# Another place for v's last tokens, and both copies of the next q and k in front of the second exp

## The chip, the cores and the metric

The kernel runs on one core of one Trainium2 chip. The metric is the device time of one execution in microseconds, and of several runs the median. TensorE is PE in the profile (PEld its weight loads), VectorE is DVE, ScalarE is ACT, GpSimd is POOL, and SyncE is SP; every load and store of this kernel is issued by SP, in the order of its queue.

## The reference

Attention over a sliding window with a linear bias, and then a mixing layer in the frequency domain on its output. The inputs are q, k, v of 8 batches × 8 heads × 576 tokens × 64, 64 pairs of complex weights of 512 × 512, and one matrix `w_ch`, all in 32 bits.

```python
scores = q @ k.T / sqrt(64)                       # per batch and head
scores = where(0 <= i - j < 128, scores - slope[h] * |i - j|, -1e9)
x = softmax(scores) @ v                           # heads side by side: (8, 576, 512)
X = rfft(x, axis=1)[:, :64]                       # 64 modes
Y = X @ (w_r + 1j * w_i)                          # each mode has its own weights
u = x + irfft(Y, n=576)
out = u + relu(u @ w_ch)
```

## The kernel before

**Units and slots.** Attention is cut into 32 units, each a pair of heads `s` of a batch `b`. Group 0 is pair 0 of the 8 batches (units 0 to 7), group 1 is pairs 1 to 3 of every batch (units 8 to 31). Unit n is worked on in slot n by `_slot` (L596), which writes out by hand, for all engines at once, the order of their instructions; nothing reorders them afterwards. In slot n:

- PE computes the first half of the scores of unit n (`_score`, L481) into the one score buffer `sc`; then 18 transposes of q and 18 of k of unit n+1 (`_tr`, L453) into `tqk`; the product of attention and v of unit n−1 (`_av`, L531 to L540); weight tiles, if the slot has any (`_modes`, L671 and L675); the second half of the scores (L481, L490); a re-ordering of v (`_keys`, L437, into `vps`); and, at the last pair of a batch, the transform into the frequency domain (`_spectrum`, L581).
- ACT takes the exp of the first half (L495), copies the transposed q of unit n+1 out of PSUM (`_evac`, L461), takes the exp of the second half, and copies the transposed k.
- DVE multiplies the attention with the mask (L505), once for each half, copies `vps` to `vb` (L441) and divides the output of unit n−1 by its sums (L545 to L551).
- POOL casts q and k of unit n+2 (`_cast_qk`, L415) and v of unit n+1 (`_cast_v`, L422) to 16 bits, and multiplies the rest of the second half with its mask (`_mask3`, L510), which the last part of `_av` in the next slot needs.

`tqk` and `vps` take turns in two PSUM buffers. So the second group of transposes for unit n+2, in slot n+1, writes the buffer that `vps` of slot n held, once DVE has copied it.

**The last tokens of v.** Tokens 512 to 575 of v have a way of their own: for each pair of heads `_load_vt` (L375) issues two loads, `_vt` casts them on POOL (L400), brings them into order with 64 products on PE (L706, from `_vt` by way of `_pair`) and copies them to `vbt` on DVE (L407). Pair 0 is taken after slot 0, and pairs 1, 2 and 3 after slots 3, 4 and 5; for those three the mask is made first (`_mask`, L302). PE's products stand behind all of slot n's PE work, and in front of slot n+1's.

**The loads.** SP's queue begins with q, k and v of the units of group 0. Then come the six loads of the last tokens of pairs 1 to 3, and then, mixed with the q, k and v of further units, the weight tiles (`_load_w`, L636): a tile is two loads, `wr` and `wi`, of 768 KB each. Each of the two has a ring of `RING` = 3 slots. The six loads of last tokens go to one slot of the ring of `wr` (the tile `vtf`), and those of pair 0 to a tile of their own in `tmpc`, a pool of temporary tiles that also holds the constants' working tiles, `ang` and `kf` among them: the angles for the transform matrix `g.F`, which DVE computes and a Sin on ACT reads. A load waits on SP until the place that it writes is free; q and k have three batches of places and v has six.

**After attention.** Group 0's 22 weight tiles are used from slot 10 on, spread over the slots; group 1's 64 tiles stream after attention has ended, with `_xw`, `_ft` and `_z_early` beside them. `_finish` computes the output and stores it.

Of the kernel before, what the change touches and what calls it, by code (L numbers as in the profile page):

```python
# [9 lines left out]
FP32 = mybir.dt.float32  # L10
# [24 lines left out]
def kernel(  # L35
# [60 lines left out]
    with tc.manual_schedule(engines={ET.SP, ET.PE, ET.Activation, ET.DVE, ET.Pool}):  # L96
        with ExitStack() as wctx:
# [4 lines left out]
            with ExitStack() as actx:  # L102
                cp = actx.enter_context(tc.tile_pool(name="const", bufs=1))
                for j, grp in enumerate(GROUPS[:-1]):
                    g.X[j] = cp.tile([P, len(grp), 3, B, NM], BF16, name=f"X{j}")
                g.mask = cp.tile([P, NP, 2, 512], BF16)
                g.vbs = [cp.tile([P, 4, 2, 72], BF16, name=f"vb{i}") for i in range(3)]
                g.vbt = cp.tile([P, NP, B, 72], BF16)
                g.sel = cp.tile([P, 2, 2, 2, 64], BF16)
                g.qpool = actx.enter_context(tc.tile_pool(name="qk", bufs=QK))  # L110
                g.vpool = actx.enter_context(tc.tile_pool(name="v", bufs=VB))
                g.vts = actx.enter_context(tc.tile_pool(name="vts", bufs=2))
                g.work = actx.enter_context(tc.tile_pool(name="work", bufs=2))
                g.ps2 = actx.enter_context(
                    tc.tile_pool(name="ps2", bufs=1, space=bass.MemoryType.PSUM))
                g.ps1 = actx.enter_context(
                    tc.tile_pool(name="ps1", bufs=2, space=bass.MemoryType.PSUM))

                todo = list(tiles[0])
                n0 = g.first[1] + LA  # L120
                with tc.tile_pool(name="tmpc", bufs=1, side="right") as tp:
                    for n in range(n0):
                        if n == g.first[1]:
                            _load_w(g, 0, *todo.pop(0))
                        _load_qk(g, n)
                        if n < VB - 1:
                            _load_v(g, n)
                        elif n >= VB + 2:
                            _load_v(g, n - 3)
                        if n == 0:  # L130
                            for s in GROUPS[0]:
                                _load_vt(g, s, tp.tile([P, 2, 4 * g.D], FP32, name=f"vtf{s}"))
                        if n == g.first[1] - 1:
                            t = g.wpool.tile([P, ROWS, DM], FP32, tag="wr", name="vtf")
                            for i, s in enumerate(GROUPS[1]):
                                _load_vt(g, s, t[:, i].rearrange("p (h c) -> p h c", h=2))
                        if g.first[1] <= n < g.first[1] + RING - 1:
                            _load_w(g, 0, *todo.pop(0))
                    _consts(g, tp)
                    _cast_qk(g, 1)  # L140
                    _cast_v(g, 0)
                    _tr(g, 0, 0)
                    _tr(g, 0, 1)
                    _evac(g, 0, 0, nc.vector.tensor_copy)
                    _evac(g, 0, 1, nc.vector.tensor_copy)
                    for s in GROUPS[0]:
                        _mask(g, s)
                    _select(g)
                    todo_s = [(0, s) for s in GROUPS[0]] + [(3 + i, s) for i, s in enumerate(GROUPS[1])]
                    for n in range(g.first[1] - 1):  # L150
                        _slot(g, n, [], [])
                        for k, s in todo_s:
                            if k == n:
                                if s not in GROUPS[0]:
                                    _mask(g, s)
                                _vt(g, tp, s)
                zx = ctx.enter_context(tc.tile_pool(name="zx", bufs=1, side="right"))
                g.ZTa = zx.tile([P, 4, 2, NM, 8], FP32)
                loaded = n0

                line = [(j, *t) for j in range(len(GROUPS)) for t in tiles[j]]
                ahead = RING
                work = {n: [] for n in range(N + 2 + TAIL)}
                for j in range(len(GROUPS) - 1):
                    steps = []
                    for n in range(g.first[j + 1] + 2, g.first[j + 2] + 2):
                        steps += [n] * (SHARE if n < N - LA else SHARE_END)
                    if j + 2 == len(GROUPS):
                        steps += [n for n in range(N + 2, N + 2 + TAIL)] * SHARE_END
                    steps.sort()  # L170
                    for i, t in enumerate(tiles[j]):
                        work[steps[i * len(steps) // len(tiles[j])]].append((j, *t))
                for n in range(g.first[1] - 1, N + 2 + TAIL):
                    if g.first[1] <= n and loaded < N + 3:
                        if loaded < N:
                            _load_qk(g, loaded)
                        _load_v(g, loaded - 3)
                        loaded += 1
                    w = work[n]
                    for _ in w:  # L180
                        _load_w(g, *line[ahead])
                        ahead += 1
                    h = (len(w) + 1) // 2
                    _slot(g, n, w[:h], w[h:])
                    for i in range(2):
# [53 lines left out]
def _consts(g, tp):  # L239
# [19 lines left out]
    nc.vector.tensor_tensor(  # L259
        out=prod, in0=scol.unsqueeze(2).broadcast_to([P, ST, NM]),  # L260
        in1=mrow.unsqueeze(1).broadcast_to([P, ST, NM]), op=ALU.mult)
    ang = tp.tile([P, ST, 2, NM], FP32)
# [3 lines left out]
    kf = tp.tile([P, ST, 2, NM], FP32)  # L266
    nc.vector.tensor_scalar(kf, ang, 1.0 / S, MAGIC, op0=ALU.mult, op1=ALU.add)
    nc.vector.tensor_scalar(kf, kf, -MAGIC, -float(S), op0=ALU.add, op1=ALU.mult)
    nc.vector.tensor_tensor(out=ang, in0=ang, in1=kf, op=ALU.add)
# [102 lines left out]
                "h (t r) d -> t h (r d)", r=4))  # L372


def _load_vt(g, s, t):  # L375


    for hh in range(2):
        g.nc.sync.dma_start(
            out=t[:, hh], in_=g.v[:, 2 * s + hh, 512:576, :].rearrange("b (t r) d -> t b (r d)", r=4))  # L380
# [12 lines left out]
        nc.gpsimd.tensor_copy(g.selt[:, :, r, r::4], src)  # L393


def _vt(g, tp, s):

    nc = g.nc
    v = tp.tile([P, 2, 4, g.D], BF16, tag="vtb", bufs=2, name=f"vtb{s}")
    nc.gpsimd.tensor_copy(v.rearrange("p h r d -> p h (r d)"), g.unit.pop(("vt", s)))  # L400
# [195 lines left out]
def _slot(g, n, w0, w1):  # L596
# [5 lines left out]
    if n + 1 < N:  # L602
        _tr(g, n + 1, 0)
        _evac(g, n + 1, 0)
        _tr(g, n + 1, 1)
    if 0 <= n - 1 < N:
        _av(g, n - 1)
    for w in w0:
        _modes(g, *w)
    if n < N:  # L610
        _score(g, n, 1)
    if n + 1 < N:
        _evac(g, n + 1, 1)
    if n + 2 < N:
        _cast_qk(g, n + 2)
    if n + 1 < N:
# [262 lines left out]
```

## Time and profile before

| | us |
|---|---|
| median of 3 runs | 488.12 |
| the three runs | 497.25, 488.12, 487.6 |
| the profiled execution | 486.97 |
| its span, first to last instruction | 485.2 |
| busy PE / DVE / ACT / POOL | 343.5 / 228.1 / 188.2 / 144.3 |

The mean granted clock of TensorE was 0.749 of full speed. The page of the profile has the busy time of each engine, the span in 40 slices of some 12 us, the chain of work that ended last, and the costliest groups of instructions. Its slices of DMA throughput:

```profile
GB/s 246 338 367 91 263 374 316 388 369 325 371 397 278 242 365 316 319 421 422 354 423 422 423 422 427 422 424 423 424 423 422 427 422 416 421 423 234 217 320 246
```

In a row of a timeline stand start, duration, engine, line and operation, output and inputs with their shapes, and in brackets how long the engine was idle before it and what ended that. In a row of the waits: who waited, for what, the sum in us, how often, and the longest. Times are counted from the span's start.

### The profile page before, as it was taken

How to read it: one execution, taken by the hardware profiler on the slowest of the kernel's cores; microseconds unless marked ns; L12 is line 12 of the kernel's file. 1: busy time of each engine (PE TensorE's matmuls, PEld its weight loads, DVE VectorE, ACT ScalarE, POOL GpSimd, SP SyncE). 2: the span in 40 equal slices, each digit the busy share in tenths (PEclk: the TensorE clock that was granted, in tenths of full speed). 3: DMA queues.
4: the chain of work that ended last, by engine and by line, in shares of the span. 5: the costliest groups of instructions: out<-in, count | busy, mean ns of one | idle time of the engine just before them, and what ended most of it. 6: DMA issues, size and time to landing. Idle time of an engine off the chain costs nothing.

```text
span 485.2 us, 14375 instructions
## 1 busy us (share of the span) xinstructions
PE 343.5 (71%) x6259; PEld 241.2 (50%) x6259; DVE 228.1 (47%) x443; ACT 188.2 (39%) x282; POOL 144.3 (30%) x189
## 2 busy tenths in 40 slices
PE   2668587897898887567674674675676569867994
PEld 1557466776776766434343332443343335634552
DVE  7365567664866557322332323224223315520884
ACT  6365556655674556111321111111112104410883
POOL 4673377666776553300000000000000000000782
PEclk9997979765896589655667556557555759988999
DMA  7992799999997799999899999999999999995587
GB/s 246 338 367 91 263 374 316 388 369 325 371 397 278 242 365 316 319 421 422 354 423 422 423 422 427 422 424 423 424 423 422 427 422 416 421 423 234 217 320 246
DMA packets 60319, 173.95 MB, mean 359 GB/s; under 512 B 4960, under 2 KB 14176, under 8 KB 60256
## 3 DMA queue, kind: packets, MB, share of 16 engines
q1 hardware_dynamic: 60256, 173.03, 92.5%
q8 instruction: 49, 0.80, 0.6%
q14 instruction: 14, 0.11, 0.1%
HBM read 163.58 MB, written 9.44 MB: 357 GB/s over the span
## 4 chain that ended last, share of the span: by engine, by line
DMA 51%; PE 21%; issue 10%; POOL 7%; ACT 4%; SPq 3%; DVE 3%; POOLq 0%; DVEq 0%; ACTq 0%
DMA wi<-in_moe_w_i_dram 40%; DMA k<-in_k_dram 5%; PE acc L675 4%; POOL qkb L415 3%; PE acc L671 3%; DMA v<-in_v_dram 3%; DMA q<-in_q_dram 2%; POOL vc L422 2%; PE sc L481 2%; PE av L531 2%; PE tqk L453 1%; PE xw L719 1%; PE mm L706 1%; PE xt L581 1%; PE tp L697 1%
## 5 line engine op out<-in xcount | busy, mean ns | idle before, releaser
L723 ACT CAST hl<-xw 64x512 bf16<-64x512 f32 x72 | 41.8, 580 | 166.3 <-PE xw L719 138.1
L675 PEld LDWEIGHTS <-wi 128*128 128x128 bf16 x1024 | 66.1, 105 | 75.7 <-DMA wi<-in_moe_w_i_dram 70.9
L845 POOL TENSOR_TENSOR o<-r,ys 128x512 f32<-128x512 f32 x18 | 22.5, 1274 | 248.1 <-DVE r L837 246.3
L495 ACT ACTIVATE att<-sc 128x1024 bf16<-128x1024 f32 x64 | 65.6, 1025 | 74.2 <-PE sc L481 35.9
L675 PE MATMUL acc<-Xlast,wi 128*128 128x16 bf16 x768 | 56.0, 193 | 51.8 <-DMA wi<-in_moe_w_i_dram 51.8
L671 PEld LDWEIGHTS <-wr 128*128 128x128 bf16 x1024 | 70.2, 107 | 41.5 <-DMA wr<-in_moe_w_r_dram 25.5
L724 DVE TENSOR_TENSOR hl<-xw,hl 64x512 bf16<-64x512 f32 x72 | 49.6, 689 | 83.8 <-ACT hl L723 83.7
L671 PE MATMUL acc<-Xlast,wr 128*128 128x16 bf16 x768 | 63.2, 194 | 23.4 <-DMA wr<-in_moe_w_r_dram 18.2
L505 DVE TENSOR_TENSOR att<-att,mask 128x1024 bf16<-128x1024 bf16 x64 | 45.2, 707 | 48.0 <-ACT att L495 47.5
L719 PE MATMUL xw<-wch,xT 128*128 128x512 bf16 x144 | 61.5, 574 | 0.0
L510 POOL TENSOR_TENSOR att<-att,mask 128x512 bf16<-128x512 bf16 x32 | 43.0, 1345 | 59.8 <-ACT att L495 56.8
L481 PE MATMUL sc<-qkT,qkT 64*64 64x256 bf16 (+1 forms) x512 | 31.3, 323 | 19.9 <-ACT qkT L461 15.5
L699 DVE COPY xT<-tp 128x512 bf16<-128x512 bf16 x36 | 15.2, 423 | 56.8 <-PE tp L697 56.6
L461 ACT COPY qkT<-tqk 128x576 bf16<-128x576 bf16 x62 | 39.4, 635 | 0.0
L453 PE MATMUL tqk<-ident_b,qkb 64*64 64x64 bf16 x1152 | 31.9, 215 | 7.9 <-ACT qkb L415 4.5
L453 PEld LDWEIGHTS <-qkb 64*64 64x64 bf16 x1152 | 31.3, 131 | 9.4 <-ACT qkb L415 4.5
L422 POOL CAST vc<-v 128x512 bf16<-128x512 f32 x32 | 27.8, 868 | 9.9 <-DMA v<-in_v_dram 9.8
L719 PEld LDWEIGHTS <-xT 128*128 128x128 bf16 x144 | 19.0, 137 | 21.9 <-issue 19.6
L437 PE MATMUL vps<-vc,sel 128*64 128x128 bf16 x512 | 24.9, 249 | 2.9 <-issue 2.7
L531 PE MATMUL av<-vb,att 128*128 128x65 bf16 x448 | 23.7, 213 | 4.4 <-POOL att L510 3.6
L481 PEld LDWEIGHTS <-qkT 64*64 64x64 bf16 x512 | 10.8, 118 | 24.8 <-ACT qkT L461 18.6
L415 POOL CAST qkb<-q 128x576 bf16<-128x576 f32 x31 | 21.5, 694 | 5.2 <-DMA q<-in_q_dram 5.2
(115 smaller groups left out, 539.5 us busy)
## 6 DMA issues: line engine op xcount, KB each, us to landing
wr<-in_moe_w_r_dram SPq DMA_DIRECT2D x85, 768.0 KB, 8.3
wi<-in_moe_w_i_dram SPq DMA_DIRECT2D x85, 768.0 KB, 9.7
v<-in_v_dram SPq DMA_DIRECT2D x64, 128.0 KB, 6.6
out_dram<-o SPq DMA_DIRECT2D x32, 256.0 KB, 2.5
q<-in_q_dram SPq DMA_DIRECT2D x9, 864.0 KB, 8.5
k<-in_k_dram SPq DMA_DIRECT2D x9, 864.0 KB, 10.2
q<-in_q_dram SPq DMA_DIRECT2D x2, 576.0 KB, 5.8
k<-in_k_dram SPq DMA_DIRECT2D x2, 576.0 KB, 6.7
```

Source lines behind the costliest of these rows:

```text
L422: g.nc.gpsimd.tensor_copy(u.vc, u.v)
L453: g.nc.tensor.transpose(tp[hs, r, :], u.b[w][hs, r], g.ident_b[hs, hs], tile_position=(64 * hh, 64 * hh))
L461: (copy or g.nc.scalar.copy)(dst.rearrange("c (p r) -> c p r", r=g.R), u.tp[w].rearrange("c r p -> c p r"))
L481: nc.tensor.matmul(sc[64 * r : 64 * r + 64, hh, c0 : c0 + nq], lhsT=kT[hs, kt * P + r : kt * P + P : 2], rhs=qT[hs, kt * P : kt * P + nq], ...
L495: nc.scalar.activation(a.rearrange("p h c -> p (h c)"), sc.rearrange("p h c -> p (h c)"), AF.Exp, scale=1.0 / math.sqrt(g.D))
L505: nc.vector.tensor_tensor(out=a, in0=a, in1=m, op=ALU.mult)
L510: g.nc.gpsimd.tensor_tensor(out=a, in0=a, in1=g.mask[:, g.units[n][1], :, 256:512], op=ALU.mult)
L671: nc.tensor.matmul(o, lhsT=wr[:, a].bitcast(BF16)[:, 1::2][:, c], rhs=X[:, a, 1:3, :, m], start=(a == 0), stop=False)
L675: nc.tensor.matmul(o, lhsT=wi[:, a].bitcast(BF16)[:, 1::2][:, c], rhs=X[:, a, 0:2, :, m], start=False, stop=(a == A - 1))
L719: nc.tensor.matmul(xw, lhsT=xT[:, dt], rhs=g.wch[:, dt], start=(dt == 0 and g.way[n] != "q"), stop=(dt == 3))
L723: nc.scalar.copy(g.hl[hi, n, h], xw[hi])
L724: nc.vector.tensor_tensor(out=g.hl[lo, n, h], in0=xw[hi], in1=g.hl[hi, n, h], op=ALU.subtract)
```

## The change

The last tokens of v leave the weights' ring. `ang` and `kf` are now allocated by name in `tmpc` ahead of the loads; the last tokens of pair 1 take the place of `kf`, those of pair 2 that of `ang`, and those of pair 0 and pair 3 share one place. The loads of pair 0 are issued with unit 1's instead of unit 0's, and the six others after the last batch of q and k of group 0, as before. The constants are emitted at that point, since their tiles have to be read before the loads take the place, and the copies of the selectors (`_select`) come right after the loads instead of after the first mask.

The cast of the last tokens is parted from the products (`_cast_vt`): for pair 0 it comes in front of the first cast of v, and for pairs 1 to 3 in front of slots 3, 4 and 5 instead of behind them. The masks and the products keep their places.

In `_slot`, the copy of k of unit n+1 comes right after the transposes of k, which puts it in front of the second exp on ACT.

```diff
                 with tc.tile_pool(name="tmpc", bufs=1, side="right") as tp:
+                    g.ang, g.kf = (
+                        tp.tile([P, ST * P], FP32, tag=t, name=t) for t in ("ang", "kf"))
                     for n in range(n0):
+                        if n == g.first[1] - 2:
+                            _consts(g, tp)
                         if n == g.first[1]:
                             _load_w(g, 0, *todo.pop(0))
                         _load_qk(g, n)
...
-                        if n == 0:
-                            for s in GROUPS[0]:
-                                _load_vt(g, s, tp.tile([P, 2, 4 * g.D], FP32, name=f"vtf{s}"))
-                        if n == g.first[1] - 1:
-                            t = g.wpool.tile([P, ROWS, DM], FP32, tag="wr", name="vtf")
-                            for i, s in enumerate(GROUPS[1]):
-                                _load_vt(g, s, t[:, i].rearrange("p (h c) -> p h c", h=2))
+                        if n == 1:
+                            _load_vt(g, tp, 0)
+                        if n == g.first[1] - 2:
+                            for s in range(1, NP):
+                                _load_vt(g, tp, s)
                         if g.first[1] <= n < g.first[1] + RING - 1:
                             _load_w(g, 0, *todo.pop(0))
-                    _consts(g, tp)
+                    _select(g)
                     _cast_qk(g, 1)
+                    _cast_vt(g, tp, 0)
                     _cast_v(g, 0)
...
-                    for s in GROUPS[0]:
-                        _mask(g, s)
-                    _select(g)
-                    todo_s = [(0, s) for s in GROUPS[0]] + [(3 + i, s) for i, s in enumerate(GROUPS[1])]
+                    _mask(g, 0)
                     for n in range(g.first[1] - 1):
+                        s = n - 2
+                        if 0 < s < NP:
+                            _cast_vt(g, tp, s)
                         _slot(g, n, [], [])
-                        for k, s in todo_s:
-                            if k == n:
-                                if s not in GROUPS[0]:
-                                    _mask(g, s)
-                                _vt(g, tp, s)
+                        if n == 0:
+                            _vt(g, 0)
+                        if 0 < s < NP:
+                            _mask(g, s)
+                            _vt(g, s)
...
-def _load_vt(g, s, t):
+def _load_vt(g, tp, s):
+    t = tp.tile([P, g.ST * P], FP32, tag=("vtf", "kf", "ang", "vtf")[s], name=f"vtf{s}")
+    t = t[:, 0 : 8 * g.D].rearrange("p (h c) -> p h c", h=2)
...
-def _vt(g, tp, s):
-    nc = g.nc
+def _cast_vt(g, tp, s):
     v = tp.tile([P, 2, 4, g.D], BF16, tag="vtb", bufs=2, name=f"vtb{s}")
-    nc.gpsimd.tensor_copy(v.rearrange("p h r d -> p h (r d)"), g.unit.pop(("vt", s)))
+    g.nc.gpsimd.tensor_copy(v.rearrange("p h r d -> p h (r d)"), g.unit.pop(("vt", s)))
+    g.unit["vtb", s] = v
+
+
+def _vt(g, s):
+    nc = g.nc
+    v = g.unit.pop(("vtb", s))
     acc = g.mpsum.tile([P, 4, 2, MB, 8], FP32, tag="acc", name="vtp")
...
         _tr(g, n + 1, 0)
         _evac(g, n + 1, 0)
         _tr(g, n + 1, 1)
+        _evac(g, n + 1, 1)
     if 0 <= n - 1 < N:
         _av(g, n - 1)
     for w in w0:
         _modes(g, *w)
     if n < N:
         _score(g, n, 1)
-    if n + 1 < N:
-        _evac(g, n + 1, 1)
     if n + 2 < N:
         _cast_qk(g, n + 2)
```

More of the change, by code (lines that the diff above doesn't have):

```diff
@@ L261, in _consts @@
         in1=mrow.unsqueeze(1).broadcast_to([P, ST, NM]), op=ALU.mult)
-    ang = tp.tile([P, ST, 2, NM], FP32)
+    ang = g.ang.rearrange("p (a r m) -> p a r m", a=ST, r=2)
     for ri in range(2):
@@ L265, in _consts @@
     MAGIC = float(2**23)
-    kf = tp.tile([P, ST, 2, NM], FP32)
+    kf = g.kf.rearrange("p (a r m) -> p a r m", a=ST, r=2)
     nc.vector.tensor_scalar(kf, ang, 1.0 / S, MAGIC, op0=ALU.mult, op1=ALU.add)
@@ L393, in _select @@
         nc.gpsimd.tensor_copy(g.selt[:, :, r, r::4], src)
-def _vt(g, tp, s):
+def _cast_vt(g, tp, s):
+    v = tp.tile([P, 2, 4, g.D], BF16, tag="vtb", bufs=2, name=f"vtb{s}")
+    g.nc.gpsimd.tensor_copy(v.rearrange("p h r d -> p h (r d)"), g.unit.pop(("vt", s)))
+    g.unit["vtb", s] = v
+def _vt(g, s):
     nc = g.nc
-    v = tp.tile([P, 2, 4, g.D], BF16, tag="vtb", bufs=2, name=f"vtb{s}")
-    nc.gpsimd.tensor_copy(v.rearrange("p h r d -> p h (r d)"), g.unit.pop(("vt", s)))
+    v = g.unit.pop(("vtb", s))
     acc = g.mpsum.tile([P, 4, 2, MB, 8], FP32, tag="acc", name="vtp")
```

## The prediction

> **What bounds the kernel now.** I read the page first, for the span and the sizes of the loads, then the waits of the DMA queue, then the windows of the stages those waits pointed to, and last the timelines of SP and POOL around the longest one. From the page:
>
> ```profile
> span 485.2 us, 14375 instructions
> ...
> wr<-in_moe_w_r_dram SPq DMA_DIRECT2D x85, 768.0 KB, 8.3
> wi<-in_moe_w_i_dram SPq DMA_DIRECT2D x85, 768.0 KB, 9.7
> v<-in_v_dram SPq DMA_DIRECT2D x64, 128.0 KB, 6.6
> out_dram<-o SPq DMA_DIRECT2D x32, 256.0 KB, 2.5
> q<-in_q_dram SPq DMA_DIRECT2D x9, 864.0 KB, 8.5
> ```
>
> Of the waits of the DMA queue, the longest single one:
>
> ```profile
> SPq L636 <- POOL vtb L400: 16.6, 1, 16.6
> ```
>
> The stages by windows (busy time of each engine, then granted clock, DMA share, GB/s):
>
> ```profile
> 30.00:35.00 5.00, 2.87 (x86) 2.32 (x80) 3.74 (x8) 4.16 (x6) 3.15 (x5) 1.00 1.05 395
> 41.20:51.00 9.80, 6.15 (x168) 5.40 (x168) 5.52 (x12) 5.64 (x9) 5.76 (x8) 0.83 0.01 3
> 75.00:150.00 75.00, 62.73 (x1572) 52.56 (x1565) 51.11 (x109) 46.50 (x61) 53.63 (x61) 0.81 0.99 359
> 150.00:200.00 50.00, 42.73 (x960) 34.92 (x959) 28.26 (x65) 24.50 (x32) 22.90 (x25) 0.74 0.86 298
> 246.00:440.00 194.00, 128.29 (x1775) 77.91 (x1776) 64.19 (x106) 39.87 (x69) 0.00 (x0) 0.66 1.02 423
> ```
>
> Three regimes. From 246 to 440 the weights stream at 423 GB/s with the queue always full: this stretch has a fixed length and starts when attention has ended (near 200), so whatever shortens attention moves the end by as much. From 75 to 200 the slots of attention set the pace and the DMA engines only just keep up. And from 41.2 to 51.0 the DMA engines are empty (3 GB/s) while every load of the kernel stands in one queue behind one wait. SP's timeline shows the place:
>
> ```profile
> 30.73 3.48 SPq L369 DMA_DIRECT2D v<-in_v_dram  x2
> 50.91 0.37 SPq L636 DMA_DIRECT2D wr<-in_moe_w_r_dram  x1
> ```
>
> The third weight tile's `wr` load needs the ring slot that holds v's last tokens; POOL reads the last of them out in slot 5. Behind that load stand v of unit 7, q and k of units 11 to 13, and v of unit 8. POOL's timeline shows what this costs the slots:
>
> ```profile
> 24.69 1.39 POOL L510 TENSOR_TENSOR att<-att,mask 128x512 bf16<-128x512 bf16 x1 [4.25 <-ACT att L495]
> ...
> 33.45 1.39 POOL L510 TENSOR_TENSOR att<-att,mask 128x512 bf16<-128x512 bf16 x1 [1.85 <-DMA k<-in_k_dram]
> 34.79 0.61 POOL L400 CAST vtb<-vtf 128x512 bf16<-128x512 f32 x1
> ...
> 48.95 1.39 POOL L510 TENSOR_TENSOR att<-att,mask 128x512 bf16<-128x512 bf16 x1 [4.04 <-ACT att L495]
> ...
> 59.62 0.61 POOL L422 CAST vc<-v 128x512 bf16<-128x512 f32 x1 [7.52 <-DMA v<-in_v_dram]
> 60.20 1.15 POOL L510 TENSOR_TENSOR att<-att,mask 128x512 bf16<-128x512 bf16 x1
> 61.29 0.66 POOL L415 CAST qkb<-q 128x576 bf16<-128x576 f32 x1
> 61.90 0.67 POOL L415 CAST qkb<-k 128x576 bf16<-128x576 f32 x1
> 64.87 0.61 POOL L422 CAST vc<-v 128x512 bf16<-128x512 f32 x1 [2.30 <-DMA v<-in_v_dram]
> ```
>
> The L510 rows are one to a slot: slot 1 at 24.69, slot 3 at 33.45, slot 5 at 48.95, slot 6 at 60.20. POOL waits 7.52 and 2.30 us for v of units 7 and 8, both held up behind the blocked load.
>
> **The change, part one: v's last tokens out of the weights' ring.** The ring's three slots are now free for three weight tiles, so the third is issued without a wait on POOL, and the queue runs on from 34. I take slot 7's cast of v (64.87) as the mark. Between the blocked load and this v stand two weight halves, two v's of two halves and one q and k: 2×768 + 4×128 + 2×864 = 3776 KB, 3.87 MB. At 395 GB/s (the row 30 to 35, the same mix of loads) that is 9.8 us; counted from 41.2, where the loads already issued have drained, v of unit 8 lands at 51.0. At 359 GB/s it would be 52.0, at 423 it would be 50.3. So the data gives 12.9 to 14.5 us, 13.9 by the nearest row.
>
> What is late next is the slots themselves: can they reach that mark by 51.0? Slots 1 to 3 took (33.45 − 24.69) / 2 = 4.4 us each; slots 3 to 5 took 7.75 each, because PE's product of the last tokens (L706, in front of the next slot's scores) waits for a cast that POOL does only after the slot's mask. Slot 0 has the same wait:
>
> ```profile
> 18.71 1.92 PE L706 MATMUL vtp<-vtb,selt 128*64 128x64 bf16 x64 [4.07 <-POOL vtb L400]
> ```
>
> The casts now stand in front of the slot's other POOL work, so these 4.07 go, and slot 1's mask comes at 20.6, slot 3's at 29.4. Slot 6's follows three slots later, each with a product of 1.92: 29.4 + 3 × (4.4 + 1.92) = 48.4. After it POOL has a mask and two casts, 1.15 + 0.66 + 0.67 = 2.5, and is at the mark at 50.9. Slots and data meet; I allow 0.4 for their not meeting exactly: **13.5 us**. If slots 3 to 5 kept 7.14 (7.75 less the cast of 0.61) and slot 0 gained nothing, slot 6's mask would come at 33.45 + 2 × 7.14 + 4.4 = 52.1 and the mark at 54.6: 10.3 us is the low end, 14.5 the high one.
>
> The smaller moves I cost at nothing. The copies of the selectors go in front of POOL's first casts, into an idle stretch at the start. The two loads of the first last-token tile go behind the second q, k and v on SP's queue, and its cast in front of POOL's first cast of v, which may hold slot 0 for a microsecond or two; the wait for v of units 6 to 8 absorbs that, and without this cover it would count in full. The last tile reuses the first one's place, so SP now waits there for POOL's first cast, with all weights queued behind; that cast is due when the second q and k have landed, before SP comes to this load. The constants are only emitted elsewhere: they issue no load, and the order on their engines stays.
>
> **Part two: both copies in front of the second exp.** ACT does, per slot, exp, copy of q, exp, copy of k; the next slot's scores need both copies and the one score buffer that the second exp frees. Around one boundary:
>
> ```profile
> 78.38 0.63 ACT L461 COPY qkT<-tqk 128x576 bf16<-128x576 bf16 x1
> 78.52 0.43 DVE L505 TENSOR_TENSOR att<-att,mask 128x512 bf16<-128x512 bf16 x1 [0.54 <-ACT att L495]
> 78.57 1.40 POOL L510 TENSOR_TENSOR att<-att,mask 128x512 bf16<-128x512 bf16 x1 [1.15 <-ACT att L495]
> 78.86 0.68 DVE L441 CAST vb<-vps 128x512 bf16<-128x512 f32 x1
> 79.07 0.14 PEld L481 LDWEIGHTS <-qkT 64*64 64x64 bf16 x8 [1.31 <-ACT qkT L461]
> 79.07 0.41 PE L481 MATMUL sc<-qkT,qkT 64*64 64x256 bf16 x8 [1.14 <-ACT qkT L461]
> 79.21 0.75 PEld L453 LDWEIGHTS <-qkb 64*64 64x64 bf16 x36
> 79.31 0.76 PE L453 MATMUL tqk<-ident_b,qkb 64*64 64x64 bf16 x36
> 79.53 1.02 ACT L495 ACTIVATE att<-sc 128x1024 bf16<-128x1024 f32 x1 [0.52 <-PE sc L481]
> ```
>
> With the copy (0.63) gone from between, the scores can start at 78.5 instead of 79.07. But not all of that arrives. PE's next work is 36 transposes, and the second 18 of them write the buffer that DVE's `vb` cast reads until 79.54: they now start near 79.6 instead of 79.31 + 0.38 = 79.7. So this slot gains 0.1, and the wait changes its name from ACT's copy to DVE's cast. Where the transposes run slowly the first 18 cover that wait:
>
> ```profile
> 101.47 1.18 PE L453 MATMUL tqk<-ident_b,qkb 64*64 64x64 bf16 x36
> ```
>
> Here 18 of them take 0.59, and about 0.5 of the 0.63 arrives. How often PE waits for this copy at all, in 75 to 183 us:
>
> ```profile
> PEld L481 <- ACT qkT L461: 13.5, 12, 1.3
> ```
>
> Twelve slots, about half of them slow by PE's rows: 6 × 0.1 + 6 × 0.5 = 3.6; I take **3**. Ends: 12 × 0.63 = 7.6 above; below nothing, since where a slot has no weight tile the second exp follows at once and now waits for a copy, 0.5 us in some seven such slots, so −3.5.
>
> The Trainium skill, page "Perfetto Trace Analysis", section "Identifying Performance Opportunities", says that improvement comes from the most-contended engine. The trace has a DMA share of 0.99 from 75 to 150, where most of the twelve slots lie; by that rule part two would give nothing there and the sum would be 13.5. The row also says 359 GB/s beside 395 in a similar mix, 9% of slack, which is why I keep 3.
>
> Sum: 13.5 + 3 = 16.5 us. The profiled execution took 486.97 with a span of 485.2; it would take 470.5. The median shown, 488.12, is 1.15 above it: **471.6**.
>
> **Rivals.** *Part two gives nothing* (0.15): the DMA engines at 0.99 take over as the bound; 13.5 alone, 474.6. *Part two gives all* (0.08): DVE's cast comes early enough, 7.6 + 13.5, 467, or 463 if slots beyond the twelve gain too. *The slots don't reach the mark* (0.14): the product on PE and the casts on POOL keep their pace, or the slots after 75 give part back; the low ends, 10.3 − 2, near 480. For it: the rows meet within 0.1 us, so there is no slack; against: 4.07 of wait clearly goes. *Slower* (0.05): the copy of k in front of the second exp delays it by 0.63 in nearly every slot, for masks on DVE and POOL and all behind them. At 31 slots that is 19.7 less 13.5: 6 us slower, 494. It decides once the second scores are ready before the copy ends in more than 13.5 / 0.63 = 21 slots. Against it: in the slots with a weight tile PE's scores come late enough to hide it. *It doesn't do what it says* (0.03): SP stops as long at the last tokens' new place, 488.
>
> **Numbers.** My forecast has 0.55. A run of this kernel tells about 2% from no change, 9.8 us, so faster means under 478.4: forecast, both part-two rivals and a third of the fourth case, 0.83. The rest of that case, the slower one (494 is 1.2%) and the last lie mostly within 2%: 0.14, and 0.03 beyond. The range runs from 463 to 480; outside it lie some 0.15.
>
> **What would show it.** SP's weight loads no longer wait on `vtb`, and there is no window under 100 GB/s between 35 and 55. Slot 7's cast of v comes near 51. PE's wait for ACT's copy in front of the scores is gone, and a wait of the transposes for `vb` stands in many slots instead. Weights from 246 on still stream at 423, starting some 16 us sooner. I am wrong if the empty window only moves, if POOL's vtb casts become what SP or PE waits for, or if the second exp waits for the copy in most slots.

## The result, and the profile after

The changed kernel took 481.12 us in the median of four runs (480.21 to 481.55); the kernel before took 492.23 beside it (487.6 to 497.25). The ratio is 0.985, with a 95% interval of 0.982 to 0.988. That is some 7 us where I had forecast 16.5, and the time lies 1 us outside my range. Here and below, a ratio leaves disturbed runs out, so it is not always the quotient of the medians beside it.

The profiled execution took 481.07 us with a span of 479.2, so 6.0 us of span are gone. The windows of the kernel after, with the same columns as before:

```profile
41.20:51.00 9.80, 7.79 (x234) 7.01 (x227) 5.05 (x11) 4.51 (x7) 3.43 (x6) 0.69 1.07 387
57.00:72.00 15.00, 12.54 (x329) 10.37 (x329) 12.06 (x26) 10.11 (x14) 11.42 (x14) 0.89 0.46 158
```

The stretch from 41.2 to 51.0, which moved 3 GB/s before, now moves 387: the blocked load is gone, as forecast. But from 57 to 72 the engines now move only 158 GB/s. In the kernel before this stretch was full:

```profile
57.00:72.00 15.00, 9.74 (x223) 7.67 (x221) 8.22 (x15) 7.07 (x10) 10.07 (x13) 0.77 1.06 380
```

The queue's waits up to 75 us in the kernel after say why. Nothing waits for `vtb` any more; the queue now stands for places that the slots themselves must free, q's and the weights':

```profile
SPq L360 <- POOL qkb L425: 8.4, 2, 8.2
SPq L645 <- PE sc L500: 6.9, 1, 6.9
```

So the loads ran ahead and the slots did not follow. POOL's timeline after, with its masks of slots 0, 3 and 6 and slot 7's cast of v, my mark:

```profile
15.67 1.39 POOL L520 TENSOR_TENSOR att<-att,mask 128x512 bf16<-128x512 bf16 x1 [0.87 <-ACT att L505]
...
33.11 1.39 POOL L520 TENSOR_TENSOR att<-att,mask 128x512 bf16<-128x512 bf16 x1 [2.80 <-ACT att L505]
...
55.10 1.16 POOL L520 TENSOR_TENSOR att<-att,mask 128x512 bf16<-128x512 bf16 x1 [3.51 <-ACT att L505]
...
57.62 1.07 POOL L432 CAST vc<-v 128x512 bf16<-128x512 f32 x1
```

I had slot 3 at 29.4, slot 6 at 48.4 and the mark at 50.9. The mark came at 57.62, and its row has no bracket: v was there, and POOL was late because of the slots. PE's waits from 17 to 56 us in the kernel after name what held them; "issue" means that the engine waited for nothing that the profile shows:

```profile
PE xt L591 <- issue: 2.6, 1, 2.6
PE av L550 <- issue: 2.0, 1, 2.0
PE vps L447 <- issue: 1.9, 1, 1.9
PE av L541 <- issue: 1.8, 1, 1.8
PE tqk L463 <- issue: 1.2, 1, 1.2
PE vtp L715 <- issue: 0.6, 1, 0.6
```

That is 10.1 us in six stops, each in front of another kind of instruction, one in the middle of the 64 products, and the view names no other wait of PE. No data and no engine explains a stop that can fall anywhere. What the stops share is their distance: in PE's timeline each stands exactly 128 products behind the one before it. From the third stop to the fourth, for example, these are 37 of the 64 products of the last tokens, then 8 + 36 + 14 + 2 + 2 + 8 + 4 + 16 products of the next slot, then one of its transform:

```profile
34.10 0.76 PE L715 MATMUL vtp<-vtb,selt 128*64 128x64 bf16 x37 [0.59 <-issue]
...
37.43 0.23 PE L591 MATMUL xt<-F,x_sb 128*128 128x128 bf16 x1
40.29 0.33 PE L591 MATMUL xt<-F,x_sb 128*128 128x128 bf16 x3 [2.64 <-issue]
```

The page of the kernel after has a queue that loads program:

```profile
PE 346.1 (72%) x6259; PEld 245.1 (51%) x6259; DVE 232.0 (48%) x443; ACT 188.9 (39%) x282; POOL 146.5 (31%) x189
...
q8 instruction: 49, 0.80, 0.6%
```

PE has 6259 products and as many weight loads, 12,518 rows of program; in 49 packets that is 255.5 rows to a packet of 16 KB. A product and its weight load are two rows, so the 128 products between two stops are 256 rows, one packet. **Theory:** PE's program comes in blocks of 256 rows through the DMA engines; a block takes longer while loads fill them; and in slots 1 to 6 PE is through its rows before the next block is there.

### The profile page after: what moved, and what is told of

The parts are those of the page before. It is cut to its first block, busy times and chain, and to the rows that moved or that the text cites. A ratio compares the mean times of both kernels' runs of the same rounds, so it can differ in the third digit from the quotient of the medians.

```text
span 479.2 us, 14419 instructions
## 1 busy us (share of the span) xinstructions
PE 346.1 (72%) x6259; PEld 245.1 (51%) x6259; DVE 232.0 (48%) x443; ACT 188.9 (39%) x282; POOL 146.5 (31%) x189
## 4 chain that ended last, share of the span: by engine, by line
DMA 54%; PE 24%; DVE 6%; ACT 5%; issue 4%; POOL 3%; SPq 2%; POOLq 0%; DVEq 0%; ACTq 0%
DMA wi<-in_moe_w_i_dram 40%; DMA k<-in_k_dram 7%; DMA v<-in_v_dram 5%; PE acc L684 4%; PE acc L680 3%; ACT att L505 3%; PE tqk L463 3%; PE av L541 2%; PE xt L591 2%; DMA vtf<-in_v_dram 2%; PE sc L491 2%; PE mm L715 1%; POOL qkb L425 1%; DVE vb L451 1%; PE xw L728 1%
## 5 line engine op out<-in xcount | busy, mean ns | idle before, releaser
L515 DVE TENSOR_TENSOR att<-att,mask 128x1024 bf16<-128x1024 bf16 x64 | 47.6, 744 | 43.0 <-ACT att L505 42.8
L463 PE MATMUL tqk<-ident_b,qkb 64*64 64x64 bf16 x1152 | 35.2, 215 | 14.4 <-DVE vb L451 8.6
L463 PEld LDWEIGHTS <-qkb 64*64 64x64 bf16 x1152 | 33.6, 131 | 17.3 <-issue 11.9
L471 ACT COPY qkT<-tqk 128x576 bf16<-128x576 bf16 x62 | 37.0, 643 | 3.4 <-PE tqk L463 3.4
L425 POOL CAST qkb<-k 128x576 bf16<-128x576 f32 x31 | 27.7, 892 | 0.6 <-DMA k<-in_k_dram 0.6
L541 PE MATMUL av<-vb,att 128*128 128x65 bf16 x448 | 22.6, 208 | 3.6 <-issue 1.8
L558 DVE TENSOR_TENSOR x_sb<-av,rec 128x512 bf16<-128x512 f32 x32 | 22.1, 692 | 0.6
L432 POOL CAST vc<-v 128x512 bf16<-128x512 f32 x32 | 22.3, 698 | 0.0
```

The lines of the kernel that those rows point to most:

```text
L425: (copy or g.nc.gpsimd.tensor_copy)(tb, t)
L463: g.nc.tensor.transpose(tp[hs, r, :], u.b[w][hs, r], g.ident_b[hs, hs], tile_position=(64 * hh, 64 * hh))
L471: (copy or g.nc.scalar.copy)(dst.rearrange("c (p r) -> c p r", r=g.R), u.tp[w].rearrange("c r p -> c p r"))
L515: nc.vector.tensor_tensor(out=a, in0=a, in1=m, op=ALU.mult)
```

## The experiments

A kernel's ratio is to the kernel before, on the chip on which it ran.

**Part one alone, and part two alone.** `e1_part1` puts the copy of k back behind the second scores; `e2_part2` is the kernel before with the copy moved.

```diff
         _tr(g, n + 1, 1)
-        _evac(g, n + 1, 1)
...
         _score(g, n, 1)
+    if n + 1 < N:
+        _evac(g, n + 1, 1)
```

> Part one alone: v's last tokens in their new place, the copy of k back behind the second scores. The theory (in slots 1 to 6 PE runs out of instructions, because each block of 256 rows of its program is fetched through the DMA engines that the loads now fill) expects that PE's idle time with no releaser between 17 and 56 us stays at 8 to 11 us, slot 6's mask at 54 to 56, the empty stretch of the DMA engines gone, and a time 2 to 3 us above that of the changed kernel: 483 to 484. The rival that part two gives nothing expects 481; the rival that part two's order is itself what holds the front slots (transposes waiting for DVE) expects the idle time to go and the time at or below 479.

> Part two alone: both copies in front of the second exp, v's last tokens still in the weights' ring. Theory: it is worth 2 to 3 us in slots 8 to 31 whatever stands in front, so 485 to 486.5 where the kernel before takes 488 to 489, and PE's idle time without a releaser in slots 1 to 6 stays near the 2 to 4 us of the kernel before. Rival (the front of the changed kernel is slow because of part two): the idle time rises to 8 us or more here as well, and the time is not better than that of the kernel before.

Part one alone: 486.7 us, ratio 0.984 (0.979 to 0.990). Part two alone: 490.25, ratio 0.989 (0.982 to 0.996). With part one alone PE's stops without a releaser remain, and the longest three are (waits from 17 to 56 us):

```profile
PE av L550 <- issue: 3.0, 1, 3.0
PE xt L591 <- issue: 2.4, 1, 2.4
PE av L541 <- issue: 1.7, 1, 1.7
```

With the smaller ones of that view, 1.1 and 0.5, they come to 8.7 us, so part two's order does not cause them. In the kernel with part two alone two remain, 1.6 and 1.1. The chip of these runs was slower (494.88 for the kernel before): both times lie above what I had expected, and what part two adds to part one can't be read from them and the changed kernel's 481.12.

**What part two is worth on top of part one.** The two kernels unchanged, on one chip: `e9_after` and `e10_part1`.

> The changed kernel itself, beside part one alone on the same chip, to settle what part two is worth on top of part one. Theory (PE's rows come at no more than 256 in some 6.1 us through the whole of attention while loads stream, so that a shorter chain between copy and score finds no rows to run): part two gives 0 to 1.5 us here, although alone it gave 1.1%. My prediction's term: 3 us.

> Part one alone once more, for the same comparison: by the theory within 1.5 us of the changed kernel; by the prediction's term 3 us above it.

The changed kernel: 482.59 us, ratio 0.979 (0.973 to 0.985). Part one alone: 486.69, 0.987 (0.981 to 0.993). The difference is 0.8%, 4 us, and the intervals overlap a little; with 1.1% for part two alone, my term of 3 us was about right, and my expectation here of 0 to 1.5, drawn from the theory for the whole of attention, was wrong. In the two profiles the difference arises late, and with it stands the granted clock (windows, first the changed kernel, then part one alone):

```profile
137.00:187.00 50.00, 43.60 (x1035) 36.31 (x1031) 31.20 (x70) 28.43 (x37) 29.83 (x33) 0.79 0.88 307
```

```profile
137.00:187.00 50.00, 44.46 (x947) 36.55 (x947) 27.78 (x61) 26.64 (x36) 27.38 (x32) 0.60 0.83 289
```

The clock was 0.79 in the one and 0.60 in the other. By the masks, slots 10 to 30 took 108.9 us in the one and 114.4 in the other. With part two alone they took 113.7, in the kernel before 111.3 (traces of other chips), so no pair of traces shows the shorter chain by itself. Whether part two works by that chain or by way of the clock is open.

**Weight tiles later.** Two kernels move the first three weight tiles back in SP's queue. The diff is that of `e3_late_w`; `e8_hold_w` has all three at `n == 14`.

```diff
-                        if n == g.first[1]:
-                            _load_w(g, 0, *todo.pop(0))
...
-                        if g.first[1] <= n < g.first[1] + RING - 1:
+                        if n in (11, 13, 15):
                             _load_w(g, 0, *todo.pop(0))
```

> The changed kernel with its first three weight tiles issued later: behind v of units 8, 10 and 12 instead of among the loads of q, k and v of units 5 to 8. The same loads in all. Theory: with fewer loads beside slots 1 to 6 the blocks of PE's program come sooner, PE's idle time without a releaser between 17 and 56 us falls from 10 to under 5, slot 6's mask comes at 50 to 52 instead of 55.1, and the time falls to 474 to 478. Rival (the stage is bound by its loads in all, or fetches have nothing to do with it): the idle time stays, slot 6's mask comes at 54 or later, and the time stays at 480 or rises to 485, because the deferred tiles are missing later.

> The changed kernel with its first three weight tiles behind q and k of units 14 to 16, so that SP stands waiting for a place for that q from about 40 us on and the DMA engines are empty in slots 4 to 6 instead of 7 to 10. Theory: in that empty stretch blocks of program come 3 to 5 us apart instead of 5 to 6.5, PE's idle time without a releaser between 38 and 57 us falls from 5.9 to under 2, slot 6's mask comes at 50 to 52 instead of 55.1, and the loads behind it start 3 to 5 us sooner than the changed kernel's (62.23): time 475 to 480 on a chip where the changed kernel takes 481. Rival: slot 6's mask stays at 54 to 56, and the time is 481 or more, since the tiles are late in slot 10.

`e3_late_w` took 481.3 us (475.6 to 487.69), ratio 0.965 (0.958 to 0.973); `e8_hold_w` took 480.06, ratio 0.981 (0.971 to 0.991). As tests of the theory both failed: other loads moved up into the gap, so the engines were as full as before, 367 GB/s from 17 to 56 in the first:

```profile
17.00:56.00 39.00, 26.68 (x779) 22.51 (x772) 23.68 (x47) 22.63 (x32) 21.06 (x28) 0.87 1.05 367
```

and 372 from 41.2 to 51.0 in the second. PE's stops remained in both (11.3 us from 17 to 56 and 10.1 from 17 to 57), as they must if full engines make them, but nothing is told apart. Slot 6's mask came at 54.59 and 51.84; the second is in the range that I expected, but the changed kernel itself had it at 52.16 in another run (`e9_after`). Why the first gained more than the changed kernel isn't settled; its runs spread by 12 us.

**The empty stretch filled in the kernel before.**

```diff
+                        if n == g.first[1] + 1:
+                            x = g.x_sb[:, 5:8].rearrange("p b t d -> p (b t d)").bitcast(FP32)
+                            y = g.X[-1].rearrange("p a r b m -> p (a r b m)").bitcast(FP32)
+                            z = g.FT.rearrange("p c s -> p (c s)").bitcast(FP32)
+                            for i, d in enumerate((
+                                    x[:, 0:1536], x[:, 1536:3072], y[:, 0:1536], z[:, 0:1024])):
+                                nc.sync.dma_start(...)
```

> The kernel before with four loads of weights (three of 768 KB, one of 512 KB) more, in front of the blocked load of the third weight tile, written to places that are unused at that time (parts of x_sb, Xlast and FT); nothing reads them, and nothing else is changed. They take some 7 of the 9.8 us in which the DMA engines were empty. Theory: blocks of PE's program that came 3 to 5 us apart between 39 and 47 now come 5 to 6.5 us apart, PE's idle time without a releaser between 36 and 60 us rises from 0.6 to 2 or more, and slot 5's mask comes at 50 to 53 instead of 48.95; time 488 to 493. Rival (fetches are not slowed by loads): the spacing, the idle time and slot 5's mask stay as they were, within 0.5 us.

One run: 499.42 us, beside 494.88 for the kernel before. From 41.2 to 51.0 it moved 242 GB/s. PE's stops without a releaser from 36 to 60 us went from 0.6 to 1.8:

```profile
PE xt L591 <- issue: 1.1, 1, 1.1
PE av L550 <- issue: 0.7, 1, 0.7
```

So they grow where only loads were added, but to no more than 1.8 where I had expected 2, and slot 5's mask came at 48.82, not later, as the rival has it: there PE has to wait for POOL's `vtb` in any case (3.0 us in this window), and that wait can hide the rest. The time lies above the 488 to 493 that I expected. By itself this run decides nothing.

**The fetch by itself.** Two small kernels: 4096 rows of transposes on PE, without and with 48 loads of weights of 768 KB beside them (`LOADS` 0 or 48, `PAIRS` 2048); all else is left out. Each ran once.

```diff
+        for i in range(LOADS):
+            nc.sync.dma_start(out=ws[i % 8]..., in_=...)
+        for i in range(PAIRS):
+            hs = slice(64 * (i % 2), 64 * (i % 2) + 64)
+            nc.tensor.transpose(tp[hs], ident[hs, hs], ident[hs, hs], ...)
```

> Only PE at work: 2048 transposes of 64x64, each a weight load and a product, 4096 rows of program or 16 blocks of 256, back to back, with no loads beside them; everything else of the kernel is left out. It measures the disputed cost by itself. Theory: a block of rows runs in 2.7 to 4 us (18 such transposes took 0.38 us), and with the DMA engines empty its fetch takes no longer than that, so the blocks come 3 to 4 us apart and PE idles less than 3 us over the whole run.

> The same 2048 transposes, with 48 loads of weights of 768 KB streaming beside them; everything else of the kernel is left out. Theory: a fetch that waits behind loads takes 5 to 7 us, so the blocks come 5 to 7 us apart while the loads run, PE idles 2 to 3 us at nearly every block, some 30 us in all, and the transposes take 80 to 110 us instead of 45 to 65. Rival (a fetch is not delayed by loads): the same spacing and the same time as without loads, within 10%.

The costliest group of each page (busy time and mean ns, then idle time before and its releaser), first without loads, then with:

```profile
L63 PE MATMUL tp<-ident 64*64 64x64 bf16 x2048 | 36.8, 196 | 21.7 <-issue 20.4
```

```profile
L63 PE MATMUL tp<-ident 64*64 64x64 bf16 x2048 | 55.1, 232 | 42.7 <-issue 41.4
```

A block is a sixteenth. Without loads it takes (36.8 + 20.4) / 16 = 3.6 us, of which PE works 2.3; with loads at some 387 GB/s it takes (55.1 + 41.4) / 16 = 6.03 us, of which PE works 3.4. The waits show one stop to each block:

```profile
PE tp L63 <- issue: 20.4, 15, 1.8
```

```profile
PE tp L63 <- issue: 41.4, 15, 3.4
```

PE's clock was lower in the second (0.62 instead of 0.99), which is why it works longer; but then it still stands 2.6 us at each block. The timeline shows that the clock does not set the distance of the blocks:

```profile
21.65 3.08 PE L63 MATMUL tp<-ident 64*64 64x64 bf16 x128 [2.68 <-issue]
28.12 3.62 PE L63 MATMUL tp<-ident 64*64 64x64 bf16 x128 [3.38 <-issue]
34.32 3.62 PE L63 MATMUL tp<-ident 64*64 64x64 bf16 x128 [2.57 <-issue]
```

The starts are 6.47 and 6.20 us apart, after 3.08 and 3.62 us of work: where PE works less, it stands longer. All such distances lie between 6.19 and 6.47 with loads and between 3.45 and 4.0 without; the 6.03 is a little lower because the first 223 products ran without a stop. In the changed kernel, with other products, the six stops end 7.56, 6.20, 6.19, 6.47 and 5.65 us apart. So the distance is the fetch, and the disputed price is 24 ns a row while loads stream.

The packets of the instruction queue, in the same two traces, say what the loads lengthen. After PE's start on a block the next packet began 1.0 to 1.3 us later without loads and 3.7 to 3.9 us later with them; the packet itself took 0.9 to 1.4 us and 1.1 us. It is the wait in front of the packet that grows, and PE, once the stops have begun, has no more than the one next block under way.

The stops without loads, 20.4 in all where I had under 3, were a miss: a quick stream of small products outruns its fetch even then.

**Fewer rows, the same time on PE.** The 64 products of pairs 1 to 3 become five of 512 columns.

```diff
+WIDE = 5
...
+    if s == 0:
         for b in range(g.B):
             for r in range(4):
                 _pair(...)
+    else:
+        for i in range(WIDE):
+            nc.tensor.matmul(acc.rearrange("p b d -> p (b d)"), lhsT=g.ident_b,
+                             rhs=v.rearrange("p h r d -> p (h r d)"), start=True, stop=True)
```

> The changed kernel with the 64 products of v's last tokens (128 rows of program, 1.92 us) replaced, for pairs 1 to 3, by five products of 512 columns with nearly the same time on PE (10 rows of program); what those three pairs get in their last tokens is therefore another value. Theory: a slot is bound by how many rows it has to fetch, so each of the three slots gets shorter by half a block's 6.2 us, 2.5 to 3 us: PE's idle time without a releaser between 17 and 56 us falls from 10 to under 5, slot 6's mask comes at 47 to 50 instead of 55.1, and the time is 4 to 7 us under that of the changed kernel. Rival (PE's work or data set the pace, not rows): slot 6's mask stays at 54 or later and the time within 1.5 us.

472.92 us, ratio 0.968 (0.959 to 0.976). POOL's timeline, the masks of slots 0 and 6 and my mark:

```profile
15.65 1.39 POOL L527 TENSOR_TENSOR att<-att,mask 128x512 bf16<-128x512 bf16 x1 [0.86 <-ACT att L512]
...
46.86 1.15 POOL L527 TENSOR_TENSOR att<-att,mask 128x512 bf16<-128x512 bf16 x1 [0.88 <-ACT att L512]
...
50.25 0.62 POOL L439 CAST vc<-v 128x512 bf16<-128x512 f32 x1 [0.82 <-DMA v<-in_v_dram]
```

PE's stops without a releaser from 17 to 56 us are down from 10.1 to 4.6. Slot 6's mask is 8.2 us sooner than in the changed kernel's profile, and now slots and data do meet: the mark stands at 50.25 and waited 0.82 us for v. I had forecast 50.9 and 51.0. The profiled span is 470.3, 14.9 under that of the kernel before; my sum was 16.5. The trace has four of the five products in 1.25 us, so five take some 1.5; the 64 took 1.39 to 1.92 in the changed kernel. PE's work was not what stood in the way; its number of rows was.

**Fewer rows in every slot.** The 16 products that re-order v become two.

```diff
-    for i in range(2):
-        for h in range(2):
-            for c in range(2):
-                for r in range(2):
-                    g.nc.tensor.matmul(o[64 * r : 64 * r + 64, i, h], ...)
+    for i in range(2):
+        g.nc.tensor.matmul(ps, lhsT=g.ident_b, rhs=u.vc.rearrange("p k c -> p (k c)"), ...)
```

> The changed kernel with the 16 products that re-order v in each slot (32 rows of program, 0.81 us of PE by the trace) replaced by two products of 512 columns with nearly the same time on PE (4 rows); v's order in attention is therefore another one. It asks whether rows bound the slots from 10 to 31 too, where PE shows hardly any idle time without a releaser. Theory: 28 rows x 31 slots = 868 rows, 3.4 blocks or 21 us less to fetch, of which the DMA engines (0.99 busy from 75 to 150) leave 8 to 15 us: slots 10 to 30 get shorter by 0.3 us or more each, and the time is 466 to 474. Rival (there PE's work and the loads set the pace): only the six front slots gain, 28 x 6 x 24 ns = 4 us, and slots 10 to 30 keep their length within 0.1 us: 477 to 481.

475.94 us, ratio 0.969 (0.964 to 0.975), between the two expectations. The masks of slots 0, 6, 10 and 30:

```profile
15.19 1.39 POOL L513 TENSOR_TENSOR att<-att,mask 128x512 bf16<-128x512 bf16 x1
...
48.44 1.15 POOL L513 TENSOR_TENSOR att<-att,mask 128x512 bf16<-128x512 bf16 x1 [2.49 <-ACT att L498]
...
68.25 1.39 POOL L513 TENSOR_TENSOR att<-att,mask 128x512 bf16<-128x512 bf16 x1 [1.43 <-ACT att L498]
...
176.04 1.40 POOL L513 TENSOR_TENSOR att<-att,mask 128x512 bf16<-128x512 bf16 x1 [3.03 <-ACT att L498]
```

Slots 10 to 30 take 107.8 us. In the changed kernel on the same chip they take 108.9:

```profile
71.96 1.39 POOL L520 TENSOR_TENSOR att<-att,mask 128x512 bf16<-128x512 bf16 x1 [1.70 <-ACT att L505]
...
180.82 1.39 POOL L520 TENSOR_TENSOR att<-att,mask 128x512 bf16<-128x512 bf16 x1 [2.81 <-ACT att L505]
```

That is 0.05 us a slot for 28 rows less: rows bound only the front slots. The wider theory, rows as the bound of all of attention, falls.

**The last tokens loaded in their final order.** The loads put v's last tokens in order, so that the products, their selectors and DVE's copy go. `e13_direct_late` also has the weight tiles of `e3_late_w`; `e14_spread` has in addition one pair's last tokens behind v of each of units 5, 6 and 7, cast a slot later.

```diff
-    t = t[:, 0 : 8 * g.D].rearrange("p (h c) -> p h c", h=2)
+    t = t[:, 0 : 8 * g.D].rearrange("p (b d) -> p b d", d=g.D)
     for hh in range(2):
         g.nc.sync.dma_start(
-            out=t[:, hh], in_=g.v[:, 2 * s + hh, 512:576, :].rearrange("b (t r) d -> t b (r d)", r=4))
+            out=t[64 * hh : 64 * hh + 64],
+            in_=g.v[:, 2 * s + hh, 512:576, :].rearrange("b t d -> t b d"))
...
-    v = tp.tile([P, 2, 4, g.D], BF16, tag="vtb", bufs=2, name=f"vtb{s}")
-    g.nc.gpsimd.tensor_copy(v.rearrange("p h r d -> p h (r d)"), g.unit.pop(("vt", s)))
-    g.unit["vtb", s] = v
+    g.nc.gpsimd.tensor_copy(g.vbt[:, s, :, 0 : g.D], g.unit.pop(("vt", s)))
```

> The changed kernel without the 64 products, the selectors and the copy on DVE for v's last tokens: their loads put the tokens in order themselves (pieces of 256 bytes instead of 1 KB) and POOL casts them straight into vbt. It computes the same. 512 rows of PE's program fewer, two blocks of some 6.2 us. Theory: slot 6's mask comes 10 to 12 us sooner than the changed kernel's 55.1, at 43 to 46, and the time is 8 to 12 us under it, 469 to 473, if the smaller pieces of the loads cost no more than 2 us. Rival (PE's busy time is what counts): 4 x 1.92 = 7.7 us of work gone, of which some is hidden: 475 or more; and if the loads of small pieces hold q, k and v up in front, 480 or more.

> The kernel with v's last tokens loaded in their final order, and in addition the first three weight tiles behind v of units 8, 10 and 12. With the rows gone, POOL stood 5.69 us in slot 4 waiting for v of unit 5, behind the loads of small pieces and two halves of a weight tile. Theory (what holds the front slots there is the order of the loads, no longer PE's rows): that wait falls to under 1.5 us, slot 6's mask comes at 43 to 46 instead of 47.88, and the time is 469 to 473. Rival (the small pieces themselves are slow, whatever follows them): the wait stays above 4 us and the time at 475 or more.

> The same, with the six loads of last tokens of pairs 1 to 3 not in one piece but one pair each behind v of units 5, 6 and 7, and their casts in front of slots 4, 5 and 6 instead of 3, 4 and 5. Theory: the front slots wait neither for rows nor for v; slot 6's mask at 42 to 45, time 467 to 472, below both kernels of this case. Rival (the stage from 75 on, at a DMA share of 0.95 to 0.98, takes back what the front gives): slot 6 as early, but the time 474 or more.

| kernel | median, us | ratio | slot 6's mask |
|---|---|---|---|
| `e11_vt_direct` | 476.27 | 0.969 (0.963 to 0.974) | 47.88 |
| `e13_direct_late` | 472.63 | 0.959 (0.951 to 0.967) | 44.83 |
| `e14_spread` | 470.38 | 0.957 (0.949 to 0.965) | 40.49 |

The first missed its 469 to 473, and its mask the 43 to 46. PE's stops are down to 0.4 us there, and a wait of POOL takes their place:

```profile
37.86 0.62 POOL L410 CAST vc<-v 128x512 bf16<-128x512 f32 x1 [5.69 <-DMA v<-in_v_dram]
```

v of unit 5 stands on SP behind the loads of small pieces and a weight tile. With the tiles later this wait is 3.06 us, with the small pieces spread it is gone, and PE's stops come to 1.4 us (from 17 to 56); the last kernel, from its masks of slots 0 and 6 and its window:

```profile
15.60 1.15 POOL L495 TENSOR_TENSOR att<-att,mask 128x512 bf16<-128x512 bf16 x1
...
40.49 1.32 POOL L495 TENSOR_TENSOR att<-att,mask 128x512 bf16<-128x512 bf16 x1
```

```profile
57.00:72.00 15.00, 12.33 (x340) 10.40 (x340) 11.05 (x25) 9.96 (x15) 11.95 (x15) 0.97 1.05 384
```

The hole from 57 to 72 is closed (384 GB/s). This kernel is faster than both kernels of this case.

**The theory in one table.** From slot 0's mask to slot 6's PE goes through six slots of 20 + 36 + 18 + 16 products (scores, transposes, the product with v, re-ordering), four times 5 of the transform, and the products of the last tokens; two rows each. At 6.03 us for 256 rows:

| kernel | rows | worked out, us | measured, us |
|---|---|---|---|
| changed kernel | 1632 | 38.4 | 55.10 − 15.67 = 39.4 |
| the same on a later chip (`e9_after`) | 1632 | 38.4 | 52.16 − 16.39 = 35.8 |
| `e12_keys_wide` | 1464 | 34.5 | 48.44 − 15.19 = 33.3 |
| `e7_vt_wide` | 1278 | 30.1 | 46.86 − 15.65 = 31.2 |
| `e14_spread` | 1120 | 26.4 | 40.49 − 15.60 = 24.9 |

They agree within 3 us, half a block. The count is no exact clock: four more kernels with 1632 rows (`e1_part1`, `e3_late_w`, `e8_hold_w`, `e10_part1`) took 36 to 39, and why the same rows took 35.8 us on one chip and 39.4 on another is not shown. Nor does it hold where something else stops the slots: `e11_vt_direct` and `e13_direct_late`, with 1120 rows like `e14_spread`, took 31.7 and 27.9, with POOL's waits for v in them.

## Why the prediction was wrong

**The failed step** is the pace of the slots in part one: "Slot 6's follows three slots later, each with a product of 1.92: 29.4 + 3 × (4.4 + 1.92) = 48.4". It prices work on PE by its duration and puts the loading of PE's program at nothing. Slot 6's mask came at 55.10. While loads stream, what counts there is rows: 180 to 190 for a slot, 4.2 to 4.5 us, near the 4.4 I took; but the 64 products are 128 rows, 128 × 6.03 / 256 = 3.0 us, not 1.92, and there is one in front of each of slots 1, 4, 5 and 6. The four of them are 4 × (3.0 − 1.92) = 4.3 of the 6.7 us by which the mask was late; the rest the count does not tell apart. From slot 3 to slot 5 it was 7.65 us a slot, nearly the 7.75 of before: the wait for the cast was gone, and stops of 0.6, 2.6 and 2.0 us had taken its place. The 1.92 was read in the kernel before off a product in front of which PE stood 4.07 us for `vtb`, time enough for its rows to come. Over half of the 6.7 us was there by slot 3, whose mask came at 33.11 instead of 29.4, in a stretch where the engines had been as full before (343 and 347 GB/s from 16 to 33). The other 3.0 came in slots 4 to 6: in the kernel before they had their fetches in the empty stretch, the very thing that part one removes. I looked for what the fuller queue would collide with among the loads, and not at the program.

Part one held in every other respect. The block on SP is gone, the data came in time, and with 354 rows fewer (`e7_vt_wide`) slots and data met at 50.25. What part one gave is 1.3 to 1.6% (0.987 and 0.984), 6 to 8 us, where I had 13.5; the whole change gave 0.985 and, in `e9_after`, 0.979, 7 to 10 us where I had 16.5. Of my rivals, the slots that don't reach the mark gave the right time, near 480, and the slots did keep their pace, but not for the cause it named: POOL's casts kept no slot waiting. That its time fits is in part luck.

My mark was also a poor one. It came 7.25 us sooner (64.87 to 57.62), but slot 8's mask only 4.3 (68.82 to 64.50): in slot 7 POOL then waited 1.52 us for ACT, where it had gone straight on before.

**Part two's term** was mis-sized by no more than the runs can tell: 3 us forecast, 4 to 5 measured (0.8% and 1.1%); in the profiles of the result, slots 10 to 30 took 108.5 us instead of 111.3. Why it gains is open, as said above. As forecast PE's wait for the copy is gone, and the waits from 75 to 183 us have new names:

```profile
PE sc L491 <- ACT att L505: 5.3, 12, 0.7
PE tqk L463 <- DVE vb L451: 5.2, 9, 1.5
```

The second is the one I named; the first is the score buffer, which the second exp frees. The rule of the Trainium skill, page "Perfetto Trace Analysis", by which improvement comes from the most-contended engine, would have made part two worth nothing, as I applied it to a DMA share of 0.99. The runs of part two alone speak against that use of it here, with the upper end of the interval at 0.996.

**Other steps.** The constants, the selectors and the first cast cost nothing, as I said: slot 0's mask came at 15.67 instead of 16.96. The wait for the second exp behind both copies did not make the kernel slower. My warning "if the empty window only moves" came true in part: 9.8 us of empty engines before, and from 57 to 72 some (395 − 158) / 395 × 15 = 9 us after. That what shortens attention moves the end by as much held nearly: slot 31's mask came 7.1 us sooner (194.30 to 187.16), the issue of the last weight load 7.7 (435.90 to 428.21), and the end of the span 6.0.

## What to carry to other kernels

When a wait or a blocked transfer is taken off the path, look at what it was hiding and what the fuller DMA engines will slow, and program is one such thing: count PE's rows in each stretch against the blocks that can come in that time. Idle time of PE that ends for no reason shown, in front of any instruction and at equal distances in rows, is the sign. In the front slots of this kernel fewer and larger products, or none, were the cure, at nearly the same time on PE; in slots 10 to 30 fewer rows gave next to nothing. A duration read beside a wait is a price with its fetch already paid.

## What the runs showed of the hardware

A block of 256 rows of short products takes PE 3.6 us with no loads beside it and 6.03 us with loads at 387 GB/s (6.2 to 6.5 from stop to stop), one stop to each block. The Trainium skill, page "Runtime: NRT & Kernel Launch", section "Instruction fetch mechanics", has the same blocks of 256 instructions, fetched through a DMA queue of the sequencer's own, and calls the cost of crossing from one to the next mostly hidden. The traces disagree for short products: 10.1 us of stops in six front slots of the changed kernel, and 41.4 of some 100 us in the small kernel with loads.
